# State-space mixer with a gated MLP: finer weight loads, the first tile pair split by parity, a second PSUM bank for the state inputs, and a new instruction order

## The chip, the cores and the metric

The kernel runs on one core of one Trainium2 chip. The metric is device time in microseconds of one execution, the median over several runs. A core has a matrix engine (TensorE, in the profile PE, with its weight loads shown apart as PEld), a vector engine (VectorE, DVE), a scalar engine (ScalarE, ACT), a general-purpose engine (GpSimd, POOL), a queue engine (SyncE, SP) that only issues transfers here, and 16 DMA engines. Matrix products land in PSUM[...]; all else lies in SBUF.

## The reference

An input x of 2048 tokens by 448 features goes through a layernorm; the result xn feeds two branches, whose product is added to x.

```
xn = layernorm(x)
# branch A: complex state space with 448 states
Lam_bar = exp(dt * Lam);  B_bar = ((Lam_bar - 1) / Lam) * B
h[t] = Lam_bar * h[t-1] + B_bar @ xn[t]
s[t] = 2 * Re(C @ h[t]) + xn[t] * Dskip
# branch B: MLP 448 -> 1792 -> 448
g = silu(gelu(layernorm(xn) @ w1 + b1) @ w2 + b2)
out = x + s * g
```

Inputs and output are bfloat16; sums of products are float32.

## The kernel before

**Tiling.** The tokens form eight blocks of 256; a block is held as 128 partitions by 2 parities (partition p has tokens 2p and 2p+1). Two blocks make a group, so there are four groups g = 0..3, and b = 0, 1 names the block in its group. The state-space branch advances two tokens at once: the scan runs over 256 token pairs per group, so its input product reads both parities (896 features, seven slices of 128), and the output for parity 1 is C times the state, while that for parity 0 uses the previous state and the token itself.

**Stages of a group.**

- Layernorm: statistics on VectorE (L357, L361), reciprocal square roots (L398 to L408, on GpSimd or VectorE), the normalised copies `xn_sb` (branch A) and `xn2_sb` (branch B) on VectorE or ScalarE (L421, L422), then transposes, by DMA issued on SP (L83, into `xnT` and `xn2T`), except for group 0's branch B, which TensorE transposes (L379, L437) and VectorE copies out (L381, L443).
- mm1 (L683; for group 0 in halves of one block each, L699): fourteen tiles of w1 in seven pairs j, each pair eight matmuls into two of the banks 0 to 3 (halves also use 4 and 5), then GELU on ScalarE (L690, L706) into `gT`.
- mm2 (L714): four per group (b, parity), each fourteen matmuls into bank 5 or 6; VectorE adds the bias (L717, `o2`), ScalarE takes a tanh (L718, `th`), VectorE makes the gate (L719, `g_sb`).
- bu (L613): the state inputs, i = 0..3. i < 3 is fourteen matmuls, i = 3 seven; all go into bank 4, which ScalarE empties into `u_sb` (L617 to L621) before the next.
- ssm: VectorE rotates u by tables (L630 to L634), scans (L638, seven per group), ScalarE narrows the result (L642 to L645), VectorE rotates back into `h_sb` (L666 to L670). GpSimd carries the last state to the next group (L652 to L664).
- ym (L746, L749, L752): the outputs, b and parity, eleven or seven matmuls into bank 7 (the last group cycles 7, 4, 0); VectorE multiplies by the gate (L755, `t3`) and adds the residual (L758, `o_sb`), which for parity 1 is `xr`, made by three operations at L730 or L731; SP stores.

Once only: 28 and 8 filling matmuls of an identity (L777); sine tables; input and output matrices of the state space turned and rotated (L564, L566; `Bn`, `BT`, `CQ`, `CZ`, called LB when the input matrix is meant); a product M0 (L602, four of them into bank 7, emptied by ScalarE at L606).

**Order.** Nothing is scheduled on the chip or when the kernel is built. The code adds tasks, each with named things it reads and writes; `ORDER` lists the task numbers in the order in which they are emitted to their engines, and `SECOND` lists the tasks that take the second of two possible engines. Each engine works through its tasks in that order and waits on semaphores where a thing it reads was written, or a thing it writes was read, elsewhere.

**Loads.** SP issues, in this order: the two parities of block 0; half of w1 (two transfers, a main part and the rest of 64 rows, `w1r`); b1; block 1; the other half of w1; the state input matrices; w2 in two; blocks 2 and 3; the output matrices. GpSimd issues `b2bc` and `dbc` (a bias and a skip vector, spread over the partitions), and halves `dbc` (L338). `fcol` says which columns of w1 make one tile: with halves of 896 columns, every seventh.

Of the kernel before, what the change touches and what calls it, by code (L numbers as in the profile page):

```python
# [13 lines left out]
PINNED = -1e5  # L14
# [132 lines left out]
0 11 18 22 12 1 9 10 19 23 14 83 16 20 24 17 2 15 5 21 25 13 27 3 26 7 8 85 6 28 4 86 29 91 40 87 30 92 84 88 93 31 89 41 94 32 43 42 44 90 48 97 95  # L147
45 33 49 47 96 50 34 59 99 108 46 51 100 110 57 109 101 102 98 35 103 52 112 58 111 53 114 113 39 137 104 116 115 105 176 140 136 106 60 117 138 55 61
118 56 139 107 177 54 141 62 120 175 146 63 119 148 67 163 64 122 142 164 65 144 68 121 161 124 69 66 147 123 71 149 126 77 150 125 81 70 152 143 128
78 154 72 74 127 153 130 73 151 129 79 36 162 132 131 303 82 155 134 75 302 76 178 266 80 307 133 305 135 309 165 167 304 145 308 306 168 310 270 179  # L150
267 156 166 171 181 169 157 172 274 180 158 170 37 314 311 315 271 316 159 312 227 160 313 278 268 38 183 272 269 282 228 275 173 273 182 285 229 317
279 318 186 174 283 280 362 230 281 184 392 320 284 231 363 321 188 286 276 364 185 232 287 277 235 319 233 365 236 366 187 234 395 237 322 368 245
367 241 189 191 243 370 369 244 192 193 323 240 371 194 195 372 197 413 324 415 374 419 417 373 196 199 200 325 375 412 416 414 203 380 418 198 420
326 204 201 238 215 239 327 202 246 213 216 205 248 421 422 328 376 424 425 219 430 206 220 255 223 256 431 257 329 214 258 259 207 381 330 224 388
377 382 208 427 383 378 242 428 379 249 247 209 250 426 389 251 252 217 253 390 384 218 254 423 210 260 221 261 222 211 262 225 472 332 212 226 474
263 473 264 385 265 331 386 288 475 333 338 476 336 334 341 478 477 289 335 342 480 479 339 340 344 482 387 337 481 391 345 291 346 343 290 347 348
349 484 350 483 292 429 293 351 393 295 352 485 356 502 357 394 294 490 296 190 358 353 354 355 359 360 297 298 491 492 486 299 361 432 523 522 526
527 525 398 487 529 488 524 528 489 433 530 399 493 494 300 434 396 505 400 397 531 534 535 401 495 536 532 496 540 435 402 541 403 405 503 404 436
497 504 537 301 538 437 406 539 600 408 438 407 441 439 542 442 498 440 533 443 446 543 450 447 449 570 544 451 448 545 571 499 455 456 444 457 453
445 458 572 452 459 460 409 546 467 574 461 573 410 462 463 466 464 454 465 547 468 575 469 576 411 470 548 471 500 552 578 577 551 553 549 579 556  # L160
580 550 561 558 582 581 554 555 559 508 501 583 562 560 564 584 557 509 563 510 506 603 511 566 585 588 512 586 513 587 507 565 515 567 568 592 589
514 569 590 516 517 591 596 593 601 594 602 595 518 597 598 609 519 599 606 520 610 521 604 611 613 605 607 608 612 617 614 621 615 618 616 619 622
620 623 624
""".split()]
SECOND = [int(k) for k in """
138 141 142 143 167 171 173 197 199 217 223 284 311 318 320 393 395 396 421 422 424 425 428 503 505 506 507 532 534 535 538 541 603
# [12 lines left out]
def bass_recurrent_scan__ssm_conv_s5__mixer_channel_mlp__prompt_kernel(  # L179
# [18 lines left out]
    with ExitStack() as es:  # L198
# [75 lines left out]
        with nc.Block():  # L274
# [38 lines left out]
            NW1 = 2  # L313

            def ldw1(c, prio):
                w = F // NW1
                ld("sp", w1_sb[:, 0:3, c * w:(c + 1) * w],
                   dram_ap(B_w1, c * w, [[F, 128], [128 * F, 3], [1, w]]), [f"w1_{c}"], 384 * w * 2, prio, dur=0.55)
                ld("sp", w1_sb[0:64, 3, c * w:(c + 1) * w], dram_ap(B_w1, 384 * F + c * w, [[F, 64], [1, w]]),
                   [f"w1r_{c}"], 64 * w * 2, prio)  # L320
# [7 lines left out]
            ldw1(1, S1 + 3)  # L328
# [4 lines left out]
            for q in range(2):  # L333
                ld("sp", w2_sb[:, q * 7:q * 7 + 7, :],
                   dram_ap(B_w2, q * 7 * 128 * D, [[7 * D, 128], [D, 7], [1, D]]), [f"w2_{q}"], 650000, S1 + 6, dur=1.7)
            ld("pool", b2bc[:], dram_ap(B_b2, 0, [[0, 128], [1, D]]), ["b2bc"], 114688, -50, reads=["sgn3"])
            ld("pool", dbc[:], dram_ap(A_Dskip, 0, [[0, 128], [1, D]]), ["dbc"], 114688, -20, reads=["b2bc"])
            pool(lambda e: e.tensor_scalar(dbc[:], dbc[:], 0.5, None, op0=ALU.mult), ["dbc"], ["dbc"], 0.8, -20)  # L338
# [25 lines left out]
            def first_norm():  # L364

                for par in range(2):
# [13 lines left out]
                                                                       ident[:, :]) for d in range(4)], [f"xm0p{par}", "ident"], [f"ps{bank}"], 0.33, 2 * PINNED)  # L380
# [227 lines left out]

            def bu(g, i, prio):
                gx = g % 2  # L610
                xk = [f"xnT{gx}_{b}" for b in range(2)]
                ms = (i, 3 + i) if i < PK else (6,)
                fns = [lambda e, r=r, m=m, d=d: e.matmul(psum[:, 4, r * NK:(r + 1) * NK], BT[:, m, d, :], xnT[:, gx, d, :],  # L613
                                                         start=(d == 0), stop=(d == 6)) for r, m in enumerate(ms) for d in range(7)]
# [249 lines left out]
```

## Time and profile before

| | |
|---|---|
| median of 13 runs | 162.13 us (160.95 to 163.99) |
| the profiled execution | 161.94 us, of which its span is 160.1 us |
| busy: TensorE, VectorE, ScalarE, GpSimd | 153.4, 133.1, 92.4, 56.7 us |
| mm2, L714, 224 matmuls | 44.5 us busy |
| mm1, L683, 168 matmuls | 38.1 us busy |
| bu, L613, 196 matmuls | 24.0 us busy |
| mm1 halves, L699, 112 matmuls | 14.2 us busy |
| ym, CZ part at L746, 56 matmuls | 11.9 us busy |
| `x_all` of blocks 2 and 3 | issued at 8.54, landed near 20.7 us |

A timeline row gives the start, the duration, the engine, the line, the operation, the tile written and the tiles read, the count, and in brackets how long the engine had stood idle before it and what ended that. Busy times of matmuls overlap (a matmul of 448 columns shows 352 ns, but fourteen of them follow each other in 2.65 us), so the pitch of a unit is taken from the chain of waits, which lists pieces in order of time.

### The profile page before, as it was taken

How to read it: one execution, taken by the hardware profiler on the slowest of the kernel's cores; microseconds unless marked ns; L12 is line 12 of the kernel's file. 1: busy time of each engine (PE TensorE's matmuls, PEld its weight loads, DVE VectorE, ACT ScalarE, POOL GpSimd, SP SyncE). 2: the span in 40 equal slices, each digit the busy share in tenths (PEclk: the TensorE clock that was granted, in tenths of full speed). 3: DMA queues.
4: the chain of work that ended last, by engine and by line, in shares of the span. 5: the costliest groups of instructions: out<-in, count | busy, mean ns of one | idle time of the engine just before them, and what ended most of it. 6: DMA issues, size and time to landing. Idle time of an engine off the chain costs nothing.

```text
span 160.1 us, 2700 instructions
## 1 busy us (share of the span) xinstructions
PE 153.4 (96%) x944; PEld 98.8 (62%) x944; DVE 133.1 (83%) x254; ACT 92.4 (58%) x152; POOL 56.7 (35%) x132
## 2 busy tenths in 40 slices
PE   6899999999999999999999999999999999999990
PEld 6689975657566665555565556567677665555560
DVE  5586998469799899699993999997989899895763
ACT  3739999949886894956289211344279678111100
POOL 5548959098200433300012833632046000005230
PEclk9999999999999999999999999999999999999999
DMA  4999999999880006000000811062601000010022
GB/s 95 330 302 395 263 176 190 137 150 180 158 188 24 0 0 131 4 0 0 0 0 17 212 35 29 0 180 58 123 4 57 0 4 0 4 54 0 27 88 59
DMA packets 29926, 14.70 MB, mean 92 GB/s; under 512 B 24597, under 2 KB 29593, under 8 KB 29914
## 3 DMA queue, kind: packets, MB, share of 16 engines
q1 hardware_dynamic: 29810, 14.31, 39.5%
q0 software_dynamic: 96, 0.23, 1.0%
q8 instruction: 7, 0.11, 0.3%
q14 instruction: 5, 0.04, 0.1%
q10 hardware_dynamic: 8, 0.00, 0.0%
HBM read 6.89 MB, written 1.84 MB: 54 GB/s over the span
## 4 chain that ended last, share of the span: by engine, by line
PE 71%; DMA 8%; SPq 4%; POOL 4%; DVE 4%; issue 4%; ACT 3%; POOLq 0%; DVEq 0%; ACTq 0%
PE psum L683 21%; PE psum L714 20%; PE psum L746 12%; PE psum L613 11%; DMA x_all<-in_A_x_dram 8%; SPq L84 4%; PE psum L749 4%; PE psum L602 3%; DVE lnst L357 1%; POOL lnw L400 1%; DVE t L755 1%; POOL dbc L338 1%; PE psum L752 1%; ACT L690 1%; ACT xn_sb L422 1%
## 5 line engine op out<-in xcount | busy, mean ns | idle before, releaser
L714 PE MATMUL psum<-w_sb,gT 128*128 128x448 bf16 x224 | 44.5, 352 | 0.0
L683 PE MATMUL psum<-xn2T,w_sb 128*128 128x512 bf16 x168 | 38.1, 380 | 0.4 <-DMA xn2T<-xn_sb 0.4
L714 PEld LDWEIGHTS psum<-w_sb,gT 128*128 128x128 bf16 x224 | 21.8, 98 | 19.4
L683 PEld LDWEIGHTS psum<-xn2T,w_sb 128*128 128x128 bf16 x168 | 21.8, 132 | 13.6 <-DMA xn2T<-xn_sb 0.7
L690 ACT ACTIVATE gT<-psum 128x1024 bf16<-128x1024 f32 x21 | 21.5, 1023 | 11.8 <-PE psum L683 11.5
L613 PE MATMUL psum<-xnT,BT 128*128 128x256 bf16 x196 | 24.0, 273 | 0.2 <-ACT u_sb L617 0.2
L613 PEld LDWEIGHTS psum<-xnT,BT 128*128 128x128 bf16 x196 | 19.1, 98 | 5.4 <-ACT u_sb L617 0.7
L718 ACT ACTIVATE th<-o 128x448 f32<-128x448 f32 x16 | 9.1, 573 | 20.7 <-DVE o L717 20.6
L755 DVE TENSOR_TENSOR t<-psum,g_sb 128x448 bf16<-128x448 f32 (+2 forms) x17 | 10.1, 591 | 5.6 <-PE psum L752 3.9
L699 PE MATMUL psum<-xn2T,w_sb 128*128 128x256 bf16 x112 | 14.2, 292 | 0.5 <-DVE xn2T L381 0.5
L638 DVE TENSOR_TENSOR_SCAN s_f<-cw,cur,v_sb 128x256 f32<-128x256 f32 x21 | 14.5, 736 | 0.2
L719 DVE SCALAR_TENSOR_TENSOR g_sb<-th,o 128x448 bf16<-128x448 f32 x16 | 10.9, 682 | 4.5 <-ACT th L718 4.5
L699 PEld LDWEIGHTS psum<-xn2T,w_sb 128*128 128x128 bf16 x112 | 12.8, 135 | 1.7 <-DVE xn2T L381 0.8
L730 POOL TENSOR_TENSOR xr<-xd,g_sb 128x448 f32<-128x448 bf16 x4 | 4.5, 1119 | 24.8 <-DVE g_sb L719 20.9
L746 PE MATMUL psum<-CZ,h_sb 128*128 128x448 bf16 x56 | 11.9, 352 | 0.0
L421 DVE TENSOR_SCALAR xn_sb<-x_all,lnw 128x448 bf16<-128x448 bf16 x20 | 10.3, 534 | 1.6 <-POOL xd L730 1.3
L717 DVE TENSOR_TENSOR o<-psum,b2bc 128x448 f32<-128x448 f32 x16 | 9.9, 617 | 2.1 <-PE psum L714 2.0
L617 ACT ACTIVATE u_sb<-psum 128x512 bf16<-128x512 f32 x12 | 7.1, 592 | 6.8 <-PE psum L613 6.8
L746 PE MATMUL psum<-CQ,h_sb 128*128 128x448 bf16 (+2 forms) x54 | 10.5, 332 | 0.0
L706 ACT ACTIVATE gT<-psum 128x512 bf16<-128x512 f32 x14 | 8.1, 592 | 3.8 <-PE psum L699 3.8
L422 ACT ACTIVATE xn_sb<-x_all,lnw 128x448 bf16<-128x448 bf16 x10 | 7.5, 754 | 4.3 <-DVE xn_sb L421 3.5
L563 ACT ACTIVATE tmp<-Cr,cw 128x448 f32<-128x448 bf16 (+1 forms) x12 | 7.9, 663 | 2.1 <-DVE CZ L566 1.7
(154 smaller groups left out, 223.5 us busy)
## 6 DMA issues: line engine op xcount, KB each, us to landing
w_sb<-in_B_w_dram SPq DMA_DIRECT2D x2, 784.0 KB, 9.3
out_dram<-tmp SPq DMA_DIRECT2D x7, 224.0 KB, 2.0
w_sb<-in_B_w_dram SPq DMA_DIRECT2D x2, 672.0 KB, 5.6
x_all<-in_A_x_dram SPq DMA_DIRECT2D x3, 448.0 KB, 3.8
gT<-in_A_C_re_dram SPq DMA_DIRECT2D x1, 392.0 KB, 12.4
Bn<-in_A_B_re_dram SPq DMA_DIRECT2D x1, 336.0 KB, 7.1
Bn<-in_A_B_im_dram SPq DMA_DIRECT2D x1, 336.0 KB, 7.3
gT<-in_A_C_im_dram SPq DMA_DIRECT2D x1, 336.0 KB, 12.6
```

The source lines that it names most:

```text
L421: on = [("dve", lambda e: e.tensor_scalar(dst, src, rs, nb, op0=ALU.mult, op1=ALU.add), 0.4, 0.12), ("act", lambda e: e.activation(dst, sr ...
L422: ("act", lambda e: e.activation(dst, src, ACT.Identity, bias=nb, scale=rs), 0.75, 0.2)]
L613: fns = [lambda e, r=r, m=m, d=d: e.matmul(psum[:, 4, r * NK:(r + 1) * NK], BT[:, m, d, :], xnT[:, gx, d, :], start=(d == 0), stop=(d == 6 ...
L638: dve(lambda e, i=i, ri=ri, init=init: e.tensor_tensor_scan(s_f[:, i, ri, :], col(R2, i).to_broadcast([128, NK]), v_sb[:, i, ri, :], init, ...
L683: fns = [lambda e, k=k, d=d: e.matmul(psum[:, b0 + k, :], w1_sb[:, d, fcol(2 * j + k)], rhs[:, d, :, :], start=(d == 0), stop=(d == 3)) fo ...
L690: act(lambda e: e.activation(gT[:, gb, 2 * j:2 * j + 2, :], psum[:, b0:b0 + 2, :], ACT.Gelu_apprx_tanh), [f"ps{b0}", f"ps{b0 + 1}"] + (WK ...
L699: fns = [lambda e, k=k, d=d: e.matmul(psum[:, banks[k], :].rearrange("p (r c) -> p r c", r=2)[:, :, cs], w1_sb[:, d, fcol(2 * j + k)], rhs ...
L714: fns = [lambda e, fi=fi: e.matmul(psum[:, bk, 0:D], gT[:, gb, fi, q * 128:(q + 1) * 128], w2_sb[:, fi, :], start=(fi == 0), stop=(fi == N ...
L717: dve(lambda e: e.tensor_tensor(o2[:, fb, :], psum[:, bk, 0:D], b2bc[:], ALU.add), [f"ps{bk}", "b2bc"], [f"oo{fb}"], 0.62, prio - 76)
L719: dve(lambda e: e.scalar_tensor_tensor(out=g_sb[:, gs, :], in0=th[:, fb, :], scalar=1.0, in1=o2[:, fb, :], op0=ALU.add, op1=ALU.mult), [f" ...
L746: fns = [lambda e, k=k: e.matmul(psum[:, bk, c0:c1], h_sb[:, hb, k, k0:k0 + 128], cm[:, k, c0:c1], start=(k == 0), stop=False) for k in ra ...
L755: dve(lambda e: e.tensor_tensor(t3[:, fb, c0:c1], psum[:, bk, c0:c1], g_sb[:, gs, c0:c1], ALU.mult), [f"ps{bk}", f"g{gs}"], [f"t3{fb}_{c0} ...
```

## The change

- w1 comes in chunks of 4, 4, 4 and 2 tiles, w2 likewise; `fcol` takes every fourth (or second) column of a chunk. `b2bc` now also waits for the last piece of w1, and `dbc` is halved on ScalarE (or VectorE).
- The 8 filling matmuls are gone; five are put behind the transposes of each parity of block 0. The first pair of mm1 for block 0 is done by parity: eight matmuls of 128 columns for each, in place of eight of 256.
- bu of groups 0 and 1 goes into bank 4 for i = 0, 2 and into bank 7 for i = 1, 3.
- In the last ym, the residual add of parity 1 may run on GpSimd, its second part is stored from ScalarE's queue, and the two parts no longer wait for each other.
- `ORDER` and `SECOND` are new throughout.

```diff
+            CH = ((0, 4), (4, 4), (8, 4), (12, 2))
             def ldw1(c, prio):
-                w = F // NW1
+                a, w = CH[c][0] * 128, CH[c][1] * 128
...
-            ld("pool", b2bc[:], dram_ap(B_b2, 0, [[0, 128], [1, D]]), ["b2bc"], 114688, -50, reads=["sgn3"])
+            ld("pool", b2bc[:], dram_ap(B_b2, 0, [[0, 128], [1, D]]), ["b2bc"], 114688, -50, reads=["sgn3", "w1r_3"])
-            pool(lambda e: e.tensor_scalar(dbc[:], dbc[:], 0.5, None, op0=ALU.mult), ["dbc"], ["dbc"], 0.8, -20)
+            kb.either(("act", lambda e: e.activation(dbc[:], dbc[:], ACT.Copy, scale=0.5), 0.6, 0.2),
+                      ("dve", lambda e: e.tensor_scalar(dbc[:], dbc[:], 0.5, None, op0=ALU.mult), 0.2, 0.12), ["dbc"], ["dbc"], -20)
...
+                    pe([lambda e: e.matmul(psum[:, 3, 0:128], ident[:, :], ident[:, :], start=True, stop=True) for _ in range(5)],
+                       [f"xm0p{par}", "ident"], ["ps3"], 0.3, 3 * PINNED + 1)
...
+                bk = 7 if g < 2 and i % 2 else 4
-                fns = [lambda e, r=r, m=m, d=d: e.matmul(psum[:, 4, r * NK:(r + 1) * NK], BT[:, m, d, :], xnT[:, gx, d, :],
+                fns = [lambda e, r=r, m=m, d=d: e.matmul(psum[:, bk, r * NK:(r + 1) * NK], BT[:, m, d, :], xnT[:, gx, d, :],
...
+                if (j, b) == (0, 0):
+                    for r in range(2):
+                        pe([lambda e, k=k, d=d, r=r: e.matmul(psum[:, banks[k], r * 256:r * 256 + 128], w1_sb[:, d, fcol(k)], xn2T[:, 0, r * 4 + d, 0:128],
+                                                              start=(d == 0), stop=(d == 3)) for k in range(2) for d in range(4)],
+                           [f"xmT0p{r}"] + wr, [f"ps{k}" for k in banks], 0.53, prio)
...
+                    if last and par:
+                        kb.either(*on, rd, [f"o{ob}_{par}_{c0}"], prio)
...
-                        kb.dma("sp", dram_ap(out, off + par * D + c0, [[2 * D, 128], [1, w]]), o_sb[:, ob, par * D + c0:par * D + c1], reads=[f"o{ob}_{par}_{c0}"],
+                        kb.dma("act" if c0 else "sp", dram_ap(out, off + par * D + c0, [[2 * D, 128], [1, w]]), o_sb[:, ob, par * D + c0:par * D + c1], reads=[f"o{ob}_{par}_{c0}"],
```

What the new lists do to TensorE's order, between group 0's mm1 and group 2's:

```
before: mm2(0) x3, bu(0), mm2(0), bu(0), mm1(1), bu(0), mm1(1), bu(0), mm1(1) x3, bu(1), mm1(1) x2,
        bu(1), mm2(1), bu(1), M0, mm2(1), bu(1), M0, mm2(1), M0, mm2(1), M0, mm1(2) x2, ym(0) ...
after:  mm2(0) x4, mm1(1) x5, M0, mm1(1), M0, bu(0), M0, mm1(1), M0, bu(0) x2, mm2(1), bu(0),
        mm2(1) x2, bu(1), mm2(1), bu(1), mm1(2), ym(0) ...
```

By the whole program, seven of the normalising passes move from VectorE to ScalarE, five of ScalarE's scalings of the output matrices move to VectorE, group 1's reciprocal square roots move from GpSimd to VectorE, and two of the `xd` and `xr` products from VectorE to GpSimd. The lines of the changed file lie a few lower (L683 is L688, L699 is L712, with L708 for the pair by parity, L714 is L723, L746 is L755, L755 is L764). SP's order after the loads is one turned input matrix, three turned output matrices, the two `xn2T` of group 1, and then the rest.

## The prediction

> **What bounds the kernel now.** I read the page's shares first, then the chain of waits, then the start and the end in the timeline. (The state-space part's input products are "bu(g,i)", the MLP's are "mm1" and "mm2", the output products "ym"; g is the group.)
>
> ```profile
> span 160.1 us, 2700 instructions
> ...
> PE 153.4 (96%) x944; PEld 98.8 (62%) x944; DVE 133.1 (83%) x254; ACT 92.4 (58%) x152; POOL 56.7 (35%) x132
> ...
> PE psum L683 21%; PE psum L714 20%; PE psum L746 12%; PE psum L613 11%; DMA x_all<-in_A_x_dram 8%; SPq L84 4%; PE psum L749 4%; PE psum L602 3%; DVE lnst L357 1%; POOL lnw L400 1%; DVE t L755 1%; POOL dbc L338 1%; PE psum L752 1%; ACT L690 1%; ACT xn_sb L422 1%
> ```
>
> TensorE is busy 96% of the span, and the last three quarters of the chain are TensorE alone, without a gap from 41.5 us to 154.7 us. VectorE, at 83%, is close behind. So a gain must come from TensorE starting sooner, from its slow phase, from its few waits, or from what follows its last product; everything else only decides whether TensorE waits.
>
> ```profile
> 7.56 5.89 PEld L699 LDWEIGHTS psum<-xn2T,w_sb 128*128 128x128 bf16 x40 [0.78 <-DVE xn2T L381]
> ...
> 7.56:10.90 3.34, 3.34 (x16) 2.46 (x17) 2.65 (x12) 0.70 (x2) 1.47 (x8) 1.00 1.08 307
> ...
> 14.00:21.70 7.70, 7.70 (x74) 7.70 (x72) 7.20 (x16) 7.13 (x13) 6.93 (x22) 1.00 1.24 284
> ```
>
> The first real product starts at 7.56 us behind a VectorE copy. In the windows (length, then PE busy and its count, and so on; PEclk is the 1.00 near the end) 16 matmuls take 3.34 us, 209 ns each, but later 74 take 7.70 us, 104 ns each: for 3.3 us they ran at half rate, although PEclk says 1.00. That costs 1.7 us.
>
> ```profile
> 42.41 5.18 PE psum L683 x24
> ...
> 36.05 1.94 PE L683 MATMUL psum<-xn2T,w_sb 128*128 128x512 bf16 x8 [0.40 <-DMA xn2T<-xn_sb]
> ...
> 38.15 1.28 ACT L690 ACT_TABLE_LOAD   x1
> 39.44 1.02 ACT L690 ACTIVATE gT<-psum 128x1024 bf16<-128x1024 f32 x1
> ...
> 41.47 0.94 PE L613 MATMUL psum<-xnT,BT 128*128 128x256 bf16 x7 [0.23 <-ACT u_sb L617]
> ...
> 154.82 0.62 DVE L755 TENSOR_TENSOR t<-psum,g_sb 128x448 bf16<-128x448 f32 x1 [1.10 <-PE psum L749]
> ...
> 156.69 0.36 DVE L755 TENSOR_TENSOR t<-psum,g_sb 128x192 bf16<-128x192 f32 x1
> 157.09 0.36 DVE L758 TENSOR_TENSOR tmp<-t,xr 128x192 bf16<-128x192 bf16 x1
> ```
>
> TensorE's only waits after the start are 0.40 and 0.23 us (in brackets), together 0.63. The chain gives its pitch per unit: 24 matmuls of mm1 in 5.18 us, so 1.73 per pair of tiles; likewise 2.65 per mm2, 1.53 and 0.77 per bu, 1.38 per m0, 2.08 and 1.33 per ym of parity 0 and 1. Its last matmul ends at 156.06; the last VectorE add at 157.45.
>
> [...]`xn_sb` normalising at L421 takes 382 ns at least, 534 on average and 1115 at most.[...]
>
> **The change part by part.**
>
> 1. First product. Before, 8 filling matmuls (5.15 to 6.18) stood ahead of both transposes. Now parity 0 (normalised at 4.76) is transposed from 5.1, behind the parameter matmuls: 4 x 0.11 to 5.5, five fillers to 6.05, parity 1 (ready 5.48) to 6.5, five fillers to 7.02. The parity 0 copy (0.42) ends near 6.2. Chunk 0 needs 0.69 MB landed (x 0.23, w1 0.46) where 1.03 MB were there before 7.5. Start 7.02: minus 0.54.
>
> 2. Slow phase. TensorE is busy without a real gap from 5.1[...]; in the profile's phase (10.9) the cost is half of 3.9, 1.9 against 1.7: plus 0.25.[...] Splitting the first pair keeps its columns: nothing.
>
> 3. Loads. Five more issues on SP at about 0.5 us delay `x_all` of blocks 2 and 3 from 8.54 to 11 in issue. It landed at 20.7, 12.2 us after issue, because the engines were full (DMA row 9 throughout), so it stays near 20.7 to 21.1. `b2bc` waits for w1's last rest (near 10); GpSimd gets there near 18: nothing. mm2 waited for both pieces of w2 and now waits for all four, the same bytes: nothing. Halving `dbc` leaves GpSimd (1.33) for ScalarE (0.6).
>
> 4. The new middle. mm2(0) now runs four in a row, then five pairs of mm1(1), before any bu. I placed the order of each engine with the trace's durations. VectorE: transposed copy at 14.9, sine arguments to 21.1, four statistics and the rsqrt steps (3.1 + 2.05) to 26.3, the first o2 add to 26.95. TensorE: halves end 21.7; the third mm2 needs that add's bank at 26.96, so it just passes; mm2 ends 32.3. The second `xn2T` transpose is issued near 28.7 and lands 3.0 to 3.2 us later, 31.9: passes. ScalarE is the late one: last two first-group GELUs to 23.4 (the argument's absolute value, 1.05, comes first, from 21.1), table load (1.28), two sines (0.84 each), a normalising pass (0.75), three sines (1.15, 0.5, 0.5) and a scaling (0.66) to 30.0, table load to 31.3, two tanh and three scalings (the last behind VectorE's LB6 at 33.9) to 34.6, a further table load to 35.9, first GELU to 36.9. mm1(1)'s third pair needs that bank and would start at 32.3 + 3.46 = 35.8: TensorE waits 1.1 us. This also swallows what a lucky phase in step 2 would give, since the statistics wait for `x_all` anyway. With no later wait, TensorE has from 36.9: 19 mm1 (32.8), 12 mm2 (31.8), bu (21.4), m0 (5.6), ym (27.2): 118.8, ending near 155.9, as before. In before's sums the same count falls 0.2 short, so 156.1.
>
> 5. Waits gone: the 0.40 (a transpose) and the 0.23 (bu's single bank) stood in the stretch that is re-ordered; step 4's placing has neither: minus 0.63.
>
> 6. State outputs. VectorE goes without idling from the CQ tables (41.3) to the first h (71.0). Its rows there: seven CZ and four scalings (0.68, 0.45: 6.6), three normalisings and two `xd` (0.39: 2.0), four gates and four o2 adds (0.62: 5.0), four statistics (3.1), one `xr` (0.6), six wide rotations (0.95: 5.7), seven scans (0.73: 5.1), four short rotations (1.4): 29.5. TensorE asks for h at 71.9: from 36.9 it has 5 mm1, 4 m0, 5.5 bu, 4 mm2 and one mm1 of group 2, 10.4 + 5.6 + 8.4 + 10.6, so 35.0. For h of group 3 it is 148.3 against 149.0. Slack 0.9 and 0.65 at my durations; groups 1 and 2: 0.6 and 1.7. Cost taken: zero. Below zero is excluded (TensorE cannot ask sooner); above, see the rivals. bu in bank 7 waits for m0's or ym's reader, each free 0.3 us or more before.
>
> 7. End. The last parity now writes 192 columns first; their add runs on GpSimd and their store on ACT's queue. VectorE after the last matmul: 0.2, then 0.41 + 0.42 and gaps: 1.07 in place of 1.39; one store fewer stands ahead on SP (0.4 us issues). Minus 0.35. GpSimd's 192-column add (estimate 0.6, from 1.1 for 448) plus its store ends sooner.
>
> Sum against the profiled execution (161.94, span 160.1): -0.54 + 0.25 - 0.63 + 1.1 - 0.35 = -0.2; the placed order, which ends TensorE at 156.1 instead of 156.06 and then saves 0.35, gives -0.3. I take that: 161.6. The median shown, 162.13, lies 0.2 above that execution, so this is 0.3% below the median.
>
> **The rivals.**
>
> Clean pass. ScalarE's run of tables is earlier than I placed it (its back-to-back instructions overlap by up to 0.1 us, 14 of them, two tanh at 30.90 take 1.04 where one takes 0.57), and step 4's 1.1 us is not paid. Then steps 1, 5 and 7 stay and some of step 2: 161.94 - 0.54 - 0.63 - 0.35 = 160.4. For it: the overlaps. Against: the extra table load, which before had 2 us of idle ScalarE in front of it.
>
> Late state outputs (the slower case). Five 448-wide GpSimd operations fall into VectorE's run to the first h, four into that to the last. In before 15 of them came with about 5.5 us of stretched VectorE work (L421 20 x 0.15, and L719, L667, L668 above their least), 0.37 each: 1.85 - 0.9 and 1.5 - 0.65 come out as 1.8 us on TensorE: 163.4. It decides from 0.31 us an operation on. For it: those stretched means; against: my rows count full durations without overlap, some 3% of 30 us.
>
> A third: the second `xn2T` lands as in before, 6.1 us after issue beside `dbc`'s load, at 34.8: then TensorE waits 2.5 instead of 1.1: 163.0. And a small chance that the two banks never matter and nothing else moves: 162.1.
>
> **How the numbers follow.** A measurement of this kernel tells about 0.5% (0.8 us) from no change. Even exchange, 161.6 (161.0 to 162.5): 0.40, of which 0.10 lie below 161.3. Clean: 0.21. Late state outputs 0.27 and late transposes 0.09: together 0.36, 0.02 of it within 0.5%. Nothing moves: 0.03. So faster 0.31, same 0.35, slower 0.34. The range must reach both sides: 160.1 to 163.7.
>
> **What would show it.** L708 starting at 7.0; [...]a TensorE wait of about 1 us at L688 on ScalarE near 36; no wait above 0.3 us at L755; the last VectorE add 1.1 us after the last matmul. I am wrong if L755 waits on VectorE for over a microsecond, or if L688 never waits.

## The result

| | before | after |
|---|---|---|
| median | 161.86 us (160.23 to 163.99, 48 runs) | 164.32 us (163.02 to 167.54, 11 runs) |
| ratio after to before | | 1.0148, 95% interval 1.0117 to 1.0180 |
| profiled execution, its span | 161.94, 160.1 us | 165.9, 164.2 us |

The change makes the kernel 1.5% slower. The forecast, 161.6 us and no measurable change, is wrong, and 164.32 lies outside its range. The profiled execution of after is one of its slow ones, 1.8 us above the median of the others (164.1), so its waits are read here for their places, and the size of the effect is taken from the others.

The page of after, shares and costliest groups (busy time, mean ns; idle before, releaser):

```profile
span 164.2 us, 2737 instructions
...
PE 152.9 (93%) x954; PEld 94.5 (58%) x954; DVE 135.5 (83%) x260; ACT 95.3 (58%) x154; POOL 57.6 (35%) x129
...
PE 59%; DVE 18%; DMA 9%; SPq 6%; ACT 3%; issue 2%; DVEq 0%; ACTq 0%
...
L755 PE MATMUL psum<-CZ,h_sb 128*128 128x448 bf16 x56 | 11.9, 353 | 0.4 <-DVE h_sb L675 0.4
```

TensorE's busy time has not grown (153.4 before); the span has, by 4.1 us. The last group answers step 6: state outputs cost 0.4 us once, not 1.8. Where the rest stands is in TensorE's timeline of after (start, duration, and in brackets the idle time before the row and what ended it):

```profile
6.92 0.64 PE L708 MATMUL psum<-xn2T,w_sb 128*128 128x128 bf16 x8
...
20.44 5.46 PE L723 MATMUL psum<-w_sb,gT 128*128 128x448 bf16 x28
27.55 5.46 PE L723 MATMUL psum<-w_sb,gT 128*128 128x448 bf16 x28 [1.65 <-DVE o L726]
34.13 3.64 PE L688 MATMUL psum<-xn2T,w_sb 128*128 128x512 bf16 x16 [1.12 <-DMA xn2T<-xn_sb]
39.67 5.35 PE L688 MATMUL psum<-xn2T,w_sb 128*128 128x512 bf16 x24 [1.90 <-ACT gT L694]
...
54.91 1.51 PE L605 MATMUL psum<-CQ,Bn 128*64 128x448 bf16 x7 [0.77 <-ACT M L609]
...
153.34 1.50 PE L755 MATMUL psum<-CZ,h_sb 128*128 128x448 bf16 x7 [0.41 <-DVE h_sb L675]
```

The start came as forecast: first product at 6.92 (forecast 7.02), mm2 at 20.44 where it was 21.84 before, 1.4 us sooner. Most of that lead is not the edit: this execution left its half-rate phase sooner. A product of 128 columns follows the last after 107 ns at half rate and after 56 ns at the full one. Eight of them take 1.03 us in before's row

```profile
5.16 1.03 PE L777 MATMUL psum<-ident 128*128 128x128 bf16 x8
```

and 0.64 us in the first row of after above. The half rate ends at 6.9 us in after and only near 10.8 in before. Then come five waits, 5.85 us together, where before had two of 0.63. The arithmetic closes: -1.40 + 5.22 = 3.8 of the 4.3 us by which TensorE's last product ends later (160.34 against 156.06).

What is late before 40 us is seen on the engines behind the loads. Timelines of after, VectorE, SP and ScalarE:

```profile
22.29 1.68 DVE L358 BATCH_NORM_STATS2 lnst<-x_all 128x6 f32<-128x448 bf16 x3 [2.70 <-DMA x_all<-in_A_x_dram]
...
26.78 0.62 DVE L726 TENSOR_TENSOR o<-psum,b2bc 128x448 f32<-128x448 f32 x1
```

```profile
11.51 0.43 SPq L84 DMA_DIRECT2D x_all<-in_A_x_dram  x1
...
25.18 3.88 SPq L83 DMA_TRANSPOSE Cr<-gT  x3
29.11 2.81 SPq L83 DMA_TRANSPOSE xn2T<-xn_sb  x2
31.96 1.31 SPq L83 DMA_TRANSPOSE Cr<-gT  x1
```

```profile
36.52 0.67 ACT L566 ACTIVATE tmp<-Cr,cw 128x448 f32<-128x448 bf16 x1 [2.41 <-DMA Cr<-gT]
37.20 1.28 ACT L694 ACT_TABLE_LOAD   x1
38.50 1.02 ACT L694 ACTIVATE gT<-psum 128x1024 bf16<-128x1024 f32 x1
```

`x_all` of blocks 2 and 3, issued at 11.51, lands at 22.3, 1.6 us later than before. VectorE stands still for it, and its ten reciprocal-root steps and the first o2 add follow; the third mm2 needs that add. On SP the first three C transposes cannot go before the C loads have landed (25.18), take 3.88 us to issue, and the two `xn2T` go out right behind them (29.11). The fourth C transpose goes last and lands at 36.4; ScalarE's product from it stands ahead of the first GELU, and TensorE waits for that GELU's bank.

### The profile page after: what moved, and what is told of

It reads as the page before. It is cut to its first block, busy times and chain, and to the rows that moved or that the text cites. A ratio compares the mean times of both kernels' runs of the same rounds, so it can differ in the third digit from the quotient of the medians.

```text
span 164.2 us, 2737 instructions
## 1 busy us (share of the span) xinstructions
PE 152.9 (93%) x954; PEld 94.5 (58%) x954; DVE 135.5 (83%) x260; ACT 95.3 (58%) x154; POOL 57.6 (35%) x129
## 4 chain that ended last, share of the span: by engine, by line
PE 59%; DVE 18%; DMA 9%; SPq 6%; ACT 3%; issue 2%; DVEq 0%; ACTq 0%
PE psum L688 15%; PE psum L723 15%; PE psum L618 12%; PE psum L755 12%; DMA x_all<-in_A_x_dram 7%; SPq L84 6%; PE psum L758 4%; DMA Cr<-gT 3%; DVE tmp L567 2%; DVE xn_sb L424 2%; DVE o L726 2%; DVE CQ L569 2%; DVE lnst L358 1%; DVE Bn L569 1%; DVE CZ L569 1%
## 5 line engine op out<-in xcount | busy, mean ns | idle before, releaser
L723 PE MATMUL psum<-w_sb,gT 128*128 128x448 bf16 x224 | 44.0, 352 | 1.6 <-DVE o L726 1.6
L688 PE MATMUL psum<-xn2T,w_sb 128*128 128x512 bf16 x168 | 39.2, 379 | 3.0 <-ACT gT L694 1.9
L723 PEld LDWEIGHTS psum<-w_sb,gT 128*128 128x128 bf16 x224 | 21.8, 98 | 21.6 <-issue 2.4
L688 PEld LDWEIGHTS psum<-xn2T,w_sb 128*128 128x128 bf16 x168 | 18.4, 111 | 19.6 <-issue 2.3
L739 POOL TENSOR_TENSOR xr<-xd,g_sb 128x448 f32<-128x448 bf16 x5 | 5.3, 1070 | 41.1 <-DVE g_sb L728 21.8
L764 DVE TENSOR_TENSOR t<-psum,g_sb 128x448 bf16<-128x448 f32 (+2 forms) x17 | 10.1, 593 | 8.3 <-PE psum L758 4.7
L425 ACT ACTIVATE xn_sb<-x_all,lnw 128x448 bf16<-128x448 bf16 x17 | 12.5, 754 | 4.7 <-POOL lnw L405 2.3
L755 PE MATMUL psum<-CZ,h_sb 128*128 128x448 bf16 x56 | 11.9, 353 | 0.4 <-DVE h_sb L675 0.4
L712 PE MATMUL psum<-xn2T,w_sb 128*128 128x256 bf16 x104 | 12.1, 273 | 0.1
L712 PEld LDWEIGHTS psum<-xn2T,w_sb 128*128 128x128 bf16 x104 | 10.9, 112 | 0.9 <-DMA w_sb<-in_B_w_dram 0.3
L358 DVE BATCH_NORM_STATS2 lnst<-x_all 128x6 f32<-128x448 bf16 x14 | 8.2, 612 | 3.4 <-DMA x_all<-in_A_x_dram 3.4
L755 PE MATMUL psum<-CQ,h_sb 128*128 128x448 bf16 (+2 forms) x54 | 10.5, 332 | 0.0
L728 DVE SCALAR_TENSOR_TENSOR g_sb<-th,o 128x448 bf16<-128x448 f32 x16 | 9.7, 613 | 0.2 <-ACT th L727 0.2
L739 POOL TENSOR_TENSOR xd<-xn_sb,dbc 128x448 bf16<-128x448 bf16 x6 | 7.3, 1222 | 4.7 <-DVE xr L740 4.3
```

The source lines that it names most:

```text
L425: ("act", lambda e: e.activation(dst, src, ACT.Identity, bias=nb, scale=rs), 0.75, 0.2)]
L688: fns = [lambda e, k=k, d=d: e.matmul(psum[:, b0 + k, :], w1_sb[:, d, fcol(2 * j + k)], rhs[:, d, :, :], start=(d == 0), stop=(d == 3)) fo ...
L712: pe([lambda e, k=k, d=d: e.matmul(psum[:, banks[k], :].rearrange("p (r c) -> p r c", r=2)[:, :, cs], w1_sb[:, d, fcol(2 * j + k)], rhs[:, ...
L723: fns = [lambda e, fi=fi: e.matmul(psum[:, bk, 0:D], gT[:, gb, fi, q * 128:(q + 1) * 128], w2_sb[:, fi, :], start=(fi == 0), stop=(fi == N ...
L739: kb.either(("pool", lambda e, o=o, i0=i0, i1=i1, op=op: e.tensor_tensor(o, i0, i1, op), 1.37, 0.15), ("dve", lambda e, o=o, i0=i0, i1=i1, ...
L755: fns = [lambda e, k=k: e.matmul(psum[:, bk, c0:c1], h_sb[:, hb, k, k0:k0 + 128], cm[:, k, c0:c1], start=(k == 0), stop=False) for k in ra ...
```

## The experiments

All ratios are to the kernel before, run beside each, with 95% intervals. Theory 1: the finer chunks make the loads late. Theory 2: the new order itself leaves its waits uncovered. Theory 3, soon added: TensorE's start is worth nothing while the loads decide when the middle can go.

A sum carries the readings. In every profile let S be the start of the first mm2, W the sum of TensorE's waits after it, and E the end of its last product. Then E - S - W is nearly the same:

| profile | S | W | E | E - S - W | ratio |
|---|---|---|---|---|---|
| before | 21.84 | 0.63 | 156.06 | 133.6 | 1 |
| after | 20.44 | 5.85 | 160.34 | 134.1 | 1.0148 (1.0117 to 1.0180) |
| old_order_1bank | 21.47 | 1.10 | 156.54 | 134.0 | 1.0066 (1.0035 to 1.0097) |
| new_order_only | 20.37 | 2.01 | 156.30 | 133.9 | 1.0127 (1.0039 to 1.0215) |
| x_first | 20.91 | 3.58 | 158.37 | 133.9 | 1.0183 (1.0128 to 1.0238) |
| x_first_cr | 21.99 | 4.48 | 161.54 | 135.1 | 1.0293 (1.0188 to 1.0399) |
| after_two_chunks | 20.80 | 2.53 | 157.27 | 133.9 | 1.0065 (1.0031 to 1.0100) |
| before_chunks | 20.09 | 3.50 | 157.68 | 134.1 | 1.0146 (1.0092 to 1.0201) |
| before_first_pair | 21.49 | 0.41 | 155.88 | 134.0 | 1.0011 (0.9985 to 1.0036) |
| before_tail | 20.62 | 1.97 | 156.33 | 133.7 | 1.0059 (1.0027 to 1.0090) |
| new_order_two_moves | 20.55 | 2.31 | 156.90 | 134.0 | 1.0127 (1.0066 to 1.0188) |
| before_early_loads | 21.61 | 0.00 | 154.86 | 133.3 | 0.9953 (0.9924 to 0.9981) |
| tail_fetch_later | 22.43 | 0.37 | 156.27 | 133.5 | 0.9988 (0.9951 to 1.0026) |
| before_fetch_sooner | 20.61 | 0.00 | 154.38 | 133.8 | 0.9973 (0.9947 to 0.9998) |
| chunks_early_loads | 22.10 | 1.93 | 157.93 | 133.9 | 1.0093 (1.0059 to 1.0128) |
| chunks_fetch_sooner | 20.35 | 2.16 | 156.70 | 134.2 | 1.0130 (1.0075 to 1.0185) |
| new_order_m_first | 21.35 | 2.89 | 158.24 | 134.0 | 1.0075 (1.0047 to 1.0104) |

So S and W hold the differences in E to within 0.9 us (133.3 to 134.2), but for x_first_cr: there the 40 products after a wait of 3.56 us take 10.16 us from 36.3 us on, and at the full-rate pitch of 216 ns for 512 columns (24 in 5.35 us in after) they would take 1.4 us less. By that estimate the first 2.8 us ran at half rate. A row is one execution, though, and ratios are not read from it: chunks_fetch_sooner ends sooner than new_order_m_first (156.70 against 158.24) and has the larger ratio. S scatters: before and before_tail are the same code up to there and have 21.84 and 20.62, so a start read from one profile shows no gain. W, too, is read once for each kernel; it tells where the waits stand.

**Edits or order, first.** The changed edits at both ends under the old `ORDER` (old_order_1bank), and the old code with the new `ORDER` and the two banks (new_order_only). Both needed the lists renumbered; two banks cannot stand under the old order, because there bu(1,1) comes ahead of readers of bank 7.

```diff
 # old_order_1bank, from after: ORDER, SECOND as before, new tasks next to their neighbours
-                bk = 7 if g < 2 and i % 2 else 4
+                bk = 4
```

> The changed kernel's edits at both ends (parity split of the first pair, five fill-ins after each transpose, w1 and w2 in four chunks, last store from ScalarE's queue) under the order of the kernel before, with state inputs in one bank. Late loads (my theory: five more issues on SP delay x_all of blocks 2 and 3 and what VectorE and ScalarE queue behind it): the lead of 1.3 us at the start comes, x_all still lands near 22.3, and part of the lead is given back at the first additions of o2; about 161.5 us, ratio to before 0.995 to 1.005. New order (rival: the middle's order is itself what costs): the lead stays whole, 160.4 us, ratio 0.99.

> The kernel before at its start and end (its loads, its first pair, its fill-ins), with the changed kernel's order in the middle and the two banks. Late loads: x_all lands near 20.7 as before, the third mm2 and the first mm1 of group 1 wait little, only ScalarE's wait for the fourth Cr transpose stays; 162 to 163.5 us, ratio 1.00 to 1.01. New order: the waits of 1.65, 1.12 and 1.90 us stay and the lead at the start is lost; 165.5 us, ratio 1.023.

Each half alone is slower: 1.0066 and 1.0127. Neither theory has it all. The order alone has 2.01 us of waits where the old one has 0.63:

```profile
31.78 3.64 PE L685 MATMUL psum<-xn2T,w_sb 128*128 128x512 bf16 x16 [0.65 <-DMA xn2T<-xn_sb]
35.70 5.36 PE L685 MATMUL psum<-xn2T,w_sb 128*128 128x512 bf16 x24 [0.28 <-ACT gT L692]
...
50.85 1.51 PE L602 MATMUL psum<-CQ,Bn 128*64 128x448 bf16 x7 [0.67 <-ACT M L606]
...
149.29 1.50 PE L748 MATMUL psum<-CZ,h_sb 128*128 128x448 bf16 x7 [0.41 <-DVE h_sb L672]
```

Those are after's waits at the same places, smaller, and without the third mm2's. In after, with later loads, they are larger; whether the loads make them so is tried next.

**One load moved in the changed kernel.** Only `ORDER` changes.

```diff
 # SP's order, from after
+x_all(2,3)
 w2_0 w2_1 w2_2 w2_3
-x_all(2,3)
 # x_first_cr, besides
+Cr(0)
 xn2T(1) xn2T(1)
-Cr(0)
```

> The changed kernel with one issue moved on SP: x_all of blocks 2 and 3 ahead of the four chunks of w2. Late loads: it lands before 20, VectorE's statistics no longer wait for it, the waits before the third mm2 (1.65) and the first mm1 of group 1 (1.12) go or shrink to under 0.5 together, ScalarE's wait for the fourth Cr transpose stays; about 162.0 us, ratio to before 1.00. New order: no change, 164.3 us, ratio 1.015. Should w2 now land after 20.4, the first mm2 would show it.

> The same, and the fourth Cr transpose issued ahead of the pair of xn2T for group 1 on SP. Late loads: as x_first, and ScalarE's product for CQ no longer waits 2.4 us on that transpose, so that the first GELU of group 1 comes before TensorE needs its banks; about 160.3 us, ratio 0.99. New order: no change, 164.3 us. If the two xn2T transposes get later by what the fourth Cr takes, the first mm1 of group 1 waits instead and the sum is as x_first.

x_first does what theory 1 says of the third mm2 (that wait is gone), and yet gains nothing. Its timelines, TensorE and SP:

```profile
20.91 10.75 PE L723 MATMUL psum<-w_sb,gT 128*128 128x448 bf16 x56
33.54 3.64 PE L688 MATMUL psum<-xn2T,w_sb 128*128 128x512 bf16 x16 [1.88 <-DMA xn2T<-xn_sb]
```

```profile
23.81 3.90 SPq L83 DMA_TRANSPOSE Cr<-gT  x3
27.75 3.70 SPq L83 DMA_TRANSPOSE xn2T<-xn_sb  x2
```

`x_all` landed at 15.4, but the C loads only near 23.8, and the three C transposes hold the queue until 27.7. The wait moved from `x_all` to the C loads. x_first_cr puts a fourth transpose there: `xn2T` goes out at 30.34, and TensorE's wait on it is 3.56 us, with none on the GELU. My expectation named this exchange as the alternative, with the sum as in x_first; 1.0293, from few runs, is no better than 1.0183.

**The parts one by one.** The changed kernel with the old two chunks, and the old kernel with one part each.

```diff
 # after_two_chunks, from after (loads, names and numbers to match)
-            CH = ((0, 4), (4, 4), (8, 4), (12, 2))
+            CH = ((0, 7), (7, 7))
 # before_chunks, from before: CH of four, fcol, w1, w2 and b2bc's wait as after, nothing else
 # before_first_pair, from before: first pair by parity, five fillers behind each transpose
 # before_tail, from before: 192 columns first, their add on GpSimd, kb.dma("act" if c0 else "sp", ...)
```

> The changed kernel with w1 and w2 loaded in two chunks each, as in the kernel before; all else (first pair by parity, fill-ins, order, two banks, end) as changed. Chunks are what makes the loads late (my theory now, beside the order's own cost of 1.4 us seen with new_order_only): x_all lands near 20 and the C loads near 22 instead of 22.3 and 25.2, the waits after the first mm2 fall from 5.9 to about 2 us as in new_order_only; fast runs near 162.2 us, ratio to before 1.005 to 1.01. Chunks are not it (the early start of the first pair crowds the loads, or the order alone): it stays near 164, ratio 1.015.

> The kernel before with w1 and w2 in four chunks each and nothing else. Chunks: five more issues on SP make x_all and the C loads about 1 us later; the cost in old_order_1bank (ratio 1.0066) is here too: 1.005 to 1.01, 162 to 163 us. Otherwise: 1.00.

> The kernel before with the first pair of tiles by parity and the two groups of five fill-ins in place of the eight, loads as before. If chunks cost what the first pair gains: the first product starts 0.5 us sooner and the gain reaches the first mm2: ratio 0.993 to 0.998. If the gain at the start is always lost at x_all: 1.00.

> The kernel before with the changed end alone: the 192 columns of the last tile first, their last addition on GpSimd, their store from ScalarE's queue. By step 7 of the prediction 0.35 us less, ratio 0.998; if the store from ScalarE's queue ends later than the span shows (the time outside the span was 1.7 to 3.1 us with old_order_1bank, 1.8 before), ratio 1.000 to 1.006.

The chunks alone cost 1.46% in the old kernel, and taking them out of the changed one brings it from 1.0148 to 1.0065, with intervals that do not meet. What is left there is the order (with the two banks, the first pair and the end). The same chunks are in old_order_1bank, under the old order beside the edits at both ends, and that costs 0.66% in all; so under the old order their cost is known to 0.7 to 1.5% only.

The first pair by parity is worth nothing measurable (1.0011), but this run does not show what a sooner start is worth, for it has none. With two chunks its first product waits for the first half of w1 and starts at 7.60 us, where before starts at 7.56:

```profile
7.60 0.63 PE L706 MATMUL psum<-xn2T,w_sb 128*128 128x128 bf16 x8 [1.18 <-DMA w_sb<-in_B_w_dram]
```

before_chunks, with the old first pair, starts at 6.82. The end alone is slower by 0.6%, where step 7 has it faster; more on it below.

In before_chunks TensorE's wait of 1.51 us at 38 leads back to a load as well. Its TensorE, ScalarE and GpSimd timelines:

```profile
37.98 1.69 PE L615 MATMUL psum<-xnT,BT 128*128 128x256 bf16 x14 [1.51 <-ACT u_sb L619]
```

```profile
36.02 0.76 ACT L422 ACTIVATE xn_sb<-x_all,lnw 128x448 bf16<-128x448 bf16 x1 [3.21 <-DVE xn_sb L421]
```

```profile
26.82 0.64 POOL L84 DMA_DIRECT2D dbc<-in_A_Dskip_dram  x1
32.41 1.34 POOL L338 TENSOR_SCALAR dbc<-dbc 128x448 bf16<-128x448 bf16 x1 [4.95 <-DMA dbc<-in_A_Dskip_dram]
```

`dbc` lands 5.5 us after its issue; `xd`, then the normalised copy that overwrites its input, then ScalarE's copy and, behind it, the eviction of bu's bank all stand in line for it. But the chunks have not made `dbc` late here. In before GpSimd's row stands at nearly the same time:

```profile
32.16 1.33 POOL L338 TENSOR_SCALAR dbc<-dbc 128x448 bf16<-128x448 bf16 x1 [3.81 <-DMA dbc<-in_A_Dskip_dram]
```

TensorE of before_chunks comes with a lead of 1.75 us (S 20.09 against 21.84), meets the same load, and after 42 us is 0.3 us behind before. So this profile shows theory 3: the lead ends at a load. Of the 1.6 us by which its last product comes later than before's, 1.20 are a wait at 117 us for a transpose of group 3, on which see the last section. That late loads are what the chunks cost is not to be read from this one profile.

What the chunks do to the load stream, over all profiles: the larger C load lands at 22.4 on average in the ten kernels with two chunks (21.6 to 23.4) and at 23.8 in the seven with four (22.7 to 24.8). `x_all` of blocks 2 and 3, where it keeps its place in the order, is issued at 8.2 to 8.8 and lands at 19.8 on average (18.0 to 20.7; nine kernels) with two, is issued at 11.4 to 11.6 and lands at 21.0 (20.1 to 22.3; four kernels) with four. The ranges overlap: before's 20.7 is the latest of its nine, and before_chunks' 20.1 is sooner than it. Rows of the DMA view of before and of after, 1.05 us a slice from 0 us:

```profile
GB/s 0 36 211 183 387 294 268 381 298 258 338 333 373 412 413 364 273 219 223 223 114 99 288 263 217 142 151 161 84 92 184 5 227 170 281 213 107 148 159 183
```

```profile
GB/s 0 32 223 234 198 217 354 304 305 292 295 324 337 372 420 381 364 242 182 230 210 103 22 130 58 175 105 136 256 218 174 178 152 48 168 162 168 161 173 198
```

In the fifth and sixth slices after moves 198 and 217 GB/s where before moves 387 and 294, and the two kinds of kernel do not overlap: from 4.2 to 6.3 us the seven kernels with four chunks move 202 to 216 GB/s, the ten with two 327 to 361. In after the queue takes 3.31 us from 3.75 us on to issue six pieces of w1, 0.55 us each, and the packets of the stretch fill 81% of the 16 engines' time, where they fill 111% in before; that the small pieces leave the engines short of work is argued from this. The bytes are the same, and the stream ends later on average, by the landings above.

**Do the loads decide what a start is worth?** The old order with the first pair by parity, and two loads sooner; and two moves on ScalarE in after_two_chunks against the order's waits.

```diff
 # before_early_loads, from before_first_pair: SP's x_all(2,3) ahead of w2, and
-            ld("pool", dbc[:], dram_ap(A_Dskip, 0, [[0, 128], [1, D]]), ["dbc"], 114688, -20, reads=["b2bc"])
+            ld("pool", dbc[:], dram_ap(A_Dskip, 0, [[0, 128], [1, D]]), ["dbc"], 114688, -20)
 # its place on GpSimd: right behind b2bc
 # new_order_two_moves, from after_two_chunks, ScalarE's order
+gelu(1, pair 1)
 tmp<-Cr
-gelu(1, pair 1)
 ...
+M02
 tmp<-Cr
-M02
```

> The kernel before with the first pair by parity and the fill-ins (as in before_first_pair), x_all of blocks 2 and 3 issued on SP ahead of w2, and the load of dbc issued on GpSimd right behind that of b2bc, not waiting for it to land. Theory: a lead of TensorE at the start is worth nothing while the loads set when the middle can begin; with the loads 1.5 to 2 us sooner the lead is kept: the waits of 0.4 each at group 1 go, ratio 0.99 to 0.996. Rival: transposes and DMA at large are full between 8 and 40 us, so a load that goes sooner makes another later: ratio 1.00 to 1.01.

> after_two_chunks (the changed kernel with w1 and w2 in two chunks) with two moves on ScalarE: the first GELU of group 1 ahead of the first product from the C transposes, and the eviction of the third block of M ahead of a state output and a product. If what the new order costs is just its waits (in after_two_chunks 0.88 on xn2T, 0.58 on ScalarE's GELU, 0.66 on M, 0.41 on h, 2.53 together, against 0.63 in the kernel before): the second and third go to under 0.2 each, 1 to 1.2 us less than after_two_chunks, 161.2 us, ratio to before 0.998 to 1.002. If the order costs by something else: no change, ratio 1.0065.

before_early_loads is faster than both kernels, 0.9953, and 0.6% better than before_first_pair, which differs from it by the two loads alone. Its profile has no TensorE wait after the first mm2; `dbc` was issued at 21.8 and landed 3.3 us later, 7 us sooner than before. TensorE's timeline there:

```profile
21.61 8.11 PE L721 MATMUL psum<-w_sb,gT 128*128 128x448 bf16 x42
...
35.26 1.91 PE L686 MATMUL psum<-xn2T,w_sb 128*128 128x512 bf16 x8
37.01 1.69 PE L616 MATMUL psum<-xnT,BT 128*128 128x256 bf16 x14
```

That fits theory 3. Its S is no sooner than in other profiles, so what is shown is that the two loads together gain 0.6% and the waits go; that a sooner start would now be kept is only argued. The waits are 0.41 of the 1.0 us by which its last product comes sooner than before_first_pair's; the rest is in the sum's constant (133.3 against 134.0), unexplained.

new_order_two_moves missed: 1.0127, and W fell from 2.53 to 2.31 only. The wait for a GELU went from the third pair to the fourth (0.70 at 37.99), because two more products from the C transposes, which share two buffers with VectorE, stood ahead of the next GELU; and the eviction still stood behind two tanh that waited 2.58 us for VectorE.

**Settling the two causes.** The early loads with four chunks; the first fillers written shorter (why, is under the last heading); and the eviction of M ahead of the two tanh.

```diff
 # chunks_early_loads: before_chunks with the two loads as in before_early_loads
 # chunks_fetch_sooner: before_chunks with
-            pe([lambda e: e.matmul(psum[:, 3, 0:128], ident[:, :], ident[:, :], start=True, stop=True) for _ in range(28)],
+            pe([lambda e: e.matmul(psum[:, 3, 0:56], ident[:, :], ident[:, 0:56], start=True, stop=True) for _ in range(64)],
 # new_order_m_first, from after_two_chunks, ScalarE's order
+M02
 tanh(1) tanh(1) u0 tmp<-Cr
-M02
```

> before_chunks (the kernel before with w1 and w2 in four chunks) with x_all of blocks 2 and 3 issued on SP ahead of w2, and the load of dbc right behind that of b2bc on GpSimd. If the chunks cost by making x_all and dbc late (the second waited for 5 us on GpSimd in before_chunks, with 1.51 us of TensorE's wait behind it): the two waits near 38 and 42 go, ratio to before 0.998 to 1.004 instead of 1.0146. If the chunks cost elsewhere: ratio above 1.01.

> before_chunks with the 28 fill-in products of 128 columns written as 64 of 56 columns, so that TensorE's instruction fetch at 114.8 us comes near 110 and not at the end of the xn2T transpose of group 3 (1.20 us of wait at 117 in before_chunks). If that coincidence is most of the chunks' cost: ratio 1.003 to 1.007 instead of 1.0146. If late loads are: it stays above 1.01.

> after_two_chunks with one move: the eviction of the third block of M ahead of the two tanh that wait for VectorE. If the new order costs by its waits alone, the 0.66 us before the fourth block of M goes and nothing takes its place: 0.65 us less, ratio 1.0025 instead of 1.0065. If tanh, now later by 0.5 us, delays g and with it VectorE's work for the state inputs: 1.0065 or more.

chunks_early_loads: 1.0093, between the two forecasts. The wait behind `dbc` is gone, but new ones stand elsewhere. Timelines, TensorE and VectorE:

```profile
22.10 8.11 PE L719 MATMUL psum<-w_sb,gT 128*128 128x448 bf16 x42 [1.71 <-ACT tmp L563]
```

```profile
25.70 0.62 DVE L722 TENSOR_TENSOR o<-psum,b2bc 128x448 f32<-128x448 f32 x1 [3.06 <-DMA b2bc<-in_B_b_dram]
```

ScalarE's last half GELU had ended at 21.2 and the last piece of w2, which now goes behind `x_all`, landed at 21.8, so the first mm2 more likely waits for w2; `b2bc` lands at 25.6. Later a bu waits 0.70 us at 38.7 for a transpose of the input matrix. With two chunks the same exchange showed no wait; with four, a load moved forward made another late. That speaks for theory 1 in its stronger form, the stream as a whole being late, though the interval of 1.0093 still meets that of before_chunks. chunks_fetch_sooner stays at 1.0130, which speaks against the coincidence described below as the chunks' cost. It does not rule it out: its profile, in which the wait at that place is 0.24 and not 1.20, is the fastest of its six runs, 1.0 us below their median.

new_order_m_first removes the wait on M, and nothing is gained (1.0075 against 1.0065): in its profile a GELU wait is 2.19 us and the state outputs of group 0 come 0.29 late. Which of the order's waits carry its cost is open; they replace each other.

## Why the prediction was wrong

- **Step 1 (first product, -0.54)** happened in after: 6.92. It takes both edits, for with two chunks the first product waits for w1 (7.60 in before_first_pair). As time it was lost: after's lead goes at the third mm2, that of before_chunks (first product 6.82) at the bu near 38 us. Step 4 even says that a lucky phase is swallowed "since the statistics wait for `x_all` anyway"; the same holds for step 1's 0.54, which the sum counted.
- **Step 2 (slow phase)** was wrong in after: the half rate ended at 6.9 us, with the last filler, and not at 10.9, the end that the step took over from before's profile. From there on it cost nothing, where the step took 1.9 us; what that gave went with step 1's lead. The end moves from profile to profile (last section); what sets it is not shown.
- **Step 3 (loads: nothing) is the step that failed.** It held that `x_all` would stay near 20.7 because the engines were full, and put the chunks' cost at nothing. There are six more issues, not five (twelve loads of w1 and w2 in place of six), and `x_all` went out at 11.51. The engines were not kept full from 4.2 to 6.3 us (81%), and the stream moved: 1.2 us for `x_all` and 1.4 for the C load on average, 1.6 and 1.9 in the profiled run. The forecast landing was close to the average of 21.0; what it was compared with, 20.7 in before's profile, was late (average 19.8). Measured, the chunks cost 0.8% under the new order (1.0148 against 1.0065) and 0.7 to 1.5% under the old. That late loads carry this is seen in the third mm2 of after, whose wait goes when `x_all` is moved (x_first); for the rest, and under the old order, it is argued.
- **Step 4 (new middle, 1.1 us)** is the second. The third mm2 was to pass with 0.01 us to spare, an estimate with no room for any delay: with late loads it waited 1.65. `xn2T` was timed by VectorE (28.7) and not by the C loads and three transposes ahead of it on SP (29.11 and 30.5), and the wait was 1.12. The GELU's wait was named rightly and sized 1.1; it was 1.90, and between 0.28 and 2.19 with two chunks. The wait before the fourth block of M, 0.51 to 0.79 in every profile of the new order but the one that moved the eviction ahead of the tanh, was not seen at all: ScalarE was placed step by step only to 36.9 us, and after that the sum said "with no later wait". (That sum has a slip that changes nothing: 36.9 and 118.8 make 155.7, not 155.9.) With the old loads the new order, with the banks, the first pair and the end, costs 0.65% (0.31 to 1.00); the smaller samples of new_order_only and new_order_two_moves give 1.3%.
- **Step 5 (-0.63)** was half right: bu does not wait in after. The wait for a transpose ahead of group 1's first mm1, 0.40 before, is there again with 1.12. No run has the new order with one bank, so what the second bank is worth is not shown.
- **Step 6 (state outputs, slack 0.65 at group 3)**: taken as zero, it cost 0.41 there in every profile of the new order, 1.06 worse than reckoned; group 0 was late once, by 0.29. The rival that put 1.8 us on GpSimd stretching VectorE does not show.
- **Step 7 (end, -0.35)**: the last VectorE add ends 0.91 after the last product (1.07 forecast, 1.39 before), and in the traces the end came: the span ends 3.6 to 4.0 us after the last product in eight of the nine profiles with the new end (4.7 in one), 4.0 to 4.4 in the eight with the old. Whether the time gains is not settled: 1.0059 for the end alone, 0.9988 with the same end and other fillers. The 0.6% of before_tail is not lost behind the span, for its runs spend 1.7 us outside it at the median, those of before 1.8; so it lies ahead of the last product.

Neither of the prediction's two signs of being wrong came: L755 waited 0.41, and L688 did wait. Both watch VectorE and ScalarE, neither the loads. The third rival, a late `xn2T` at 163.0 us, had the right place and chance 0.09; its cause, `dbc`'s load beside it, was not the one seen. Chunks (before_chunks) and order (after_two_chunks) alone sum to 2.1%, together they cost 1.5%. Their intervals just allow a plain sum; that both act on the same stretch before 55 us, and a wait for one hides part of the other, is argued.

## What to carry to other kernels

A sooner start of the bottleneck engine was worth here only what the next thing it met, a load stream, let through (before_chunks' lead of 1.75 us was gone at 42 us): test it by moving the loads, not by the time of the first product, which also differs where the code up to it is the same (7.56 us in before, 6.87 in before_tail). A transfer that is said to be "hidden because the engines are full" deserves a look at the bytes moved slice by slice, since here six small issues early went with loads that landed a microsecond later. And where a hand-placed order passes with less slack than the scatter of a load from profile to profile (over 2 us here: `x_all` at 18.0 to 20.7), count the wait, not the pass.

## What the runs showed of the hardware

**The half-rate phase.** It is read from the pitch of the products (107 and 56 ns for 128 columns, 213 and 109 for 256), for PEclk shows 1.00 in the first phase, as in the prediction's window from 7.56 to 10.90. The two profiles in which half rate comes back later have the lowest mean clock of the seventeen, 0.985 in tail_fetch_later and 0.99 in x_first_cr; the others have 0.997 to 1.000. The first fillers start at 1.4 us in all seventeen profiles. The first phase ends between 4.1 and 7.0 us in fourteen of them and between 9.7 and 10.8 in three (before, before_early_loads, old_order_1bank); tail_fetch_later, at full rate by 6.35 us (eight fillers in 0.62 us), falls back to half rate after 8.05: 40 products take 6.24 us from there, and 40 take 4.53 at full rate in chunks_fetch_sooner, so by estimate for 3.4 us. These four have S from 21.5 to 22.4; nine of the other thirteen have it from 20.1 to 20.9, the other four from 21.35 to 22.1.

**A transpose that lands late.** before_tail's 1.97 us of waits hold one of 1.40 us at 116 us, far from its edit:

```profile
116.02 1.91 PE L684 MATMUL psum<-xn2T,w_sb 128*128 128x512 bf16 x8 [1.40 <-DMA xn2T<-xn_sb]
```

TensorE there waits for group 3's second `xn2T` transpose, which landed 4.9 us after its issue where it lands after 3.2 in the profile of before. In before_tail an instruction fetch (queue q8 of the DMA view) falls 2.8 us after that issue, beside the transpose's end; in before it comes 6.6 us after. I took the fetch for the cause and for one of TensorE's instructions, both assumptions that nothing here shows, and changed the number of TensorE's instructions ahead of it.

```diff
 # tail_fetch_later: before_tail with the 28 fillers of 128 columns as 14 of 256
 # before_fetch_sooner: before with the 28 fillers of 128 columns as 64 of 56
```

> before_tail with the first 28 fill-in products of 128 columns on TensorE written as 14 of 256 columns: the same time, 14 matrix products fewer, so each later fetch of TensorE's instructions comes 14 products later (that at 113.8 us near 115.5). If the fetch beside the last bytes of the xn2T transpose is what makes that transpose land 4.9 us after its issue instead of 3.1 (1.40 us of wait at 116): the wait goes, ratio 0.995 to 1.000 instead of 1.0059. If it is the store on ScalarE's queue or the order of the end: ratio stays 1.006.

> The kernel before with the 28 fill-in products of 128 columns written as 64 of 56 columns: about the same time, 36 products more, so the fetch at 118.75 us comes near 114. If a fetch there delays the transpose: TensorE waits 1 to 1.5 us on xn2T at 116, ratio 1.004 to 1.009. If not: 1.00. The other fetches move too (those at 28 to 35 us among the first transposes), which can cost or gain there.

In tail_fetch_later the wait is gone and the ratio back at 0.9988, as that theory asked; but the fetch, at 115.4 us where before_tail has it at 113.8, had hardly moved against the transpose (3.0 us after the issue, 2.8 in before_tail), and the transpose landed after 3.1 us beside it. So the gain is not shown to come from the fetch. In before_fetch_sooner it came at 109 us (118.8 in before), ahead of the issue, not near 114, so that run did not try what it was meant to; it waits nowhere.

Over ten profiles of the old order the landing has two values: 4.7 to 4.9 us in before_tail, before_chunks and chunks_early_loads, 3.1 to 3.2 in the other seven. All three late landings have a fetch 2.4 to 2.8 us after the issue, but three of the prompt ones have it nearly there (2.8 to 3.0 us: before_first_pair, before_early_loads, tail_fetch_later). A fetch went with every late landing and did not always bring one. What sets the landing stays open, and with it whether the changed end costs anything. It was worth 1.2 to 1.4 us of TensorE's time where it struck.
